# Bias stage of an attention and MoE kernel: two fp16 coefficient parts, three pairs of switch tiles by 16-bit distance, two blocks per chunk on ScalarE and GpSimd

## The chip, the cores and the metric

The kernel runs on one core of a Trainium2 chip. The metric is device time in microseconds (us), the median of several executions. One further execution was taken with the hardware profiler; all rows below are from that one.

## The reference, cut to what matters

An attention (batch 4, 8 heads, sequence 576, head size 64) whose scores get a bias from a small network of the position distance, then a gated MoE layer over the 2304 tokens of width 512.

```python
rel = (pos[:, None] - pos[None, :]).astype(np.float32)
x = (np.log1p(np.abs(rel)) / psi_i)[..., None]
h = np.maximum(x @ w1 + b1, 0.0)          # 32 hidden units
bias = h @ w2                             # one value per head
scores = scale * q @ k.T + bias.transpose(2, 0, 1)[None]
attn = exp(scores - max); attn = attn / (sum + 1e-9)
out = (sigmoid(y @ w_gate) * (y @ w_val)) @ w_out   # y = attn @ v, all heads side by side
```

All in fp32. The bias has 8 x 576 x 576 values and does not depend on the batch.

## The kernel before, in words

Three stages follow each other on the same engines: the bias stage, the attention over 16 units (4 head pairs x 4 batches), and the MoE. The order of every engine's instructions is the order in which the code writes them.

The bias stage uses that a ReLU is a switch times a line: for each pair of positions and each hidden unit a switch tile holds 1 where the unit is on, and bias = x * (sum of switch * w1 * w2) + (sum of switch * b1 * w2). The stage runs over 9 chunks of 64 query positions. A chunk has 16 switch tiles of 4 queries x 32 hidden units on the partitions and 576 keys in the free dimension, and 5 blocks of keys, taken in the order 0, 1, 4, 2, 3 (`BORD`): four of 128 keys with 16 groups of sums each, and block 4 with 64 keys and 8 groups.

- Twelve tiles of a chunk (`OWN`) come from TensorE: `one` makes y by two matmuls of 288 columns (line 332) into a PSUM tile, and ScalarE (line 337, a very steep sigmoid) or in chunk 0 partly VectorE (line 335) turns it into a bf16 switch. Two pairs (`DPAIRS`, tiles 6, 7, 14, 15) come from VectorE by comparing fp16 distances with fp16 thresholds (`apart`, line 350): one instruction of 1024 elements per pair and one of 256 for the rest ("far").
- `sums` (line 356) multiplies a switch tile as the stationary operand with the coefficients `cfs`, 64 columns, in three bf16 parts: three matmuls per group, 72 groups per chunk.
- `leave` takes a block out of its PSUM tile (`bps`, two buffers): VectorE multiplies the first half with x (line 364, or line 377 for block 4) into `btmp`, then adds the second half into the bias tiles by two instructions (line 372, heads 0 to 5 and 6 to 7). For block 0 (not in the last chunk) and block 4, ScalarE copies the second half (line 367) and GpSimd adds (lines 372 and 382).
- The y tiles and far pieces of the next chunk are placed between the sums by the tables `YPOS` and `DPOS` (a number is 16 x the block's place + the group).
- After every block `conv` runs a step of a preparation of nine MoE weight blocks: per block an absolute value on ScalarE (line 201) and four VectorE instructions on 512 elements (lines 204, 207, 210 and 213). From the second chunk on about one of these VectorE instructions follows each block.

The attention's softmax (line 567) reads the bias tiles on VectorE. Quoted from `leave` and the loop:

```python
if blk in BPOOL and c < NCH - 1 or blk == 4:
    rest, add = tp.tile([128, 2, H, 32], F32, name="brest")[:, 0:n], nc.gpsimd
    nc.scalar.activation(out=rest, in_=ps[:, 0:n, 1], func=AF.Copy)
else:
    rest, add = ps[:, 0:n, 1], nc.vector
```

In what follows block 1's eviction on VectorE (its multiply and two adds) is called E1, block 2's E2 and block 3's E3.

Of the kernel before, what the change touches and what calls it, by code (L numbers as in the profile page):

```python
# [31 lines left out]
YPOS = [18, 22, 26, 30, 34, 38, 46, 52, 57, 62, 67, 72], [3, 9, 15, 21, 27, 33, 39, 45, 52, 58, 66, 72]  # L32
DPAIRS = range(6, 8)
# [115 lines left out]
def tile_kernel(ctx, tc, q, k, v, small, w_gate, w_val, w_out, steps, lpos, xtab, lx, out, phases="0AB"):  # L149
# [8 lines left out]
    with ExitStack() as right, ExitStack() as att:  # L158
# [7 lines left out]
        biases = over.tile([128, 24, S], F32, name="bias0"), keep.tile([128, 8, S], F32, name="bias3")  # L166
# [1016 lines left out]
```

## Time and profile before

| | |
|---|---|
| median of 3 runs | 803.83 us (803.63 to 804.48) |
| profiled execution, its own time | 804.37 us |
| its span | 802.6 us |
| TensorE matmul busy in the span | 774.0 us (96%) |
| VectorE | 634.8 us (79%) |
| ScalarE | 511.5 us (64%) |
| GpSimd | 343.7 us (43%) |
| bias stage: first sums at | 15.07 us |
| first softmax of the attention at | 108.26 us |

Busy shares are over the whole span. The bias stage is the first eighth of it, and there the four engines hand tiles to each other through few buffers, so the times at which one instruction starts after another say more than the shares. In a timeline row the first number is the start, the second the duration, both in us, and a bracket gives the idle time before it and what ended it. Neighbouring instructions of one engine overlap a little, so the distance between two starts (the pitch) is what an instruction costs in a row of them.

### The profile page before, as it was taken

What the parts mean: (1) busy time and instruction counts of PE and PEld (TensorE: products, weight loads), DVE (VectorE), ACT (ScalarE), POOL (GpSimd) and SP (SyncE); (2) the same over time, 40 slices, a digit from 0 to 9 for tenths busy, and PEclk for the clock granted to TensorE, in tenths of its full rate; (3) what the DMA queues carried; (4) which work ended last, traced back from release to release, by engine and by line L of the source; (5) the groups of instructions that cost most, each with busy time, mean ns of one, the idle gap of its engine ahead of it and who ended that gap; (6) DMA issues with size and microseconds to landing.
All of it is one profiled execution on the core that took longest, in us unless ns stands there. A gap on an engine that the chain in (4) does not pass through costs nothing.

```text
span 802.6 us, 17329 instructions
## 1 busy us (share of the span) xinstructions
PE 774.0 (96%) x6356; PEld 722.8 (90%) x6356; DVE 634.8 (79%) x1301; ACT 511.5 (64%) x1094; POOL 343.7 (43%) x400
## 2 busy tenths in 40 slices
PE   7999989999999998899999999999999999999997
PEld 4888879999999998888998999889999999999996
DVE  6788888999999999896799899877877865656542
ACT  5888769989989987784444443554545546444442
POOL 1233559999989998951000000126233231523200
PEclk8999999999999999999999999999999999999999
DMA  5543434654664667747999633376334306321202
GB/s 198 152 147 126 130 97 125 176 167 131 180 172 127 180 178 205 212 125 234 367 313 297 203 132 131 118 220 220 111 106 145 105 27 212 129 73 64 75 1 79
DMA packets 66693, 124.21 MB, mean 155 GB/s; under 512 B 7344, under 2 KB 28976, under 8 KB 66608
## 3 DMA queue, kind: packets, MB, share of 16 engines
q1 hardware_dynamic: 64688, 120.15, 48.8%
q10 hardware_dynamic: 1920, 2.95, 1.2%
q8 instruction: 50, 0.82, 0.4%
q14 instruction: 35, 0.29, 0.1%
HBM read 86.04 MB, written 27.60 MB: 142 GB/s over the span
## 4 chain that ended last, share of the span: by engine, by line
PE 73%; DVE 13%; ACT 5%; DMA 4%; issue 3%; SPq 1%; POOL 0%; ACTq 0%; DVEq 0%
PE po L916 16%; PE pg L1018 12%; PE pu L1018 9%; PE sc L563 8%; PE acc L648 7%; PE pt L586 6%; PE pu L892 4%; PE pg L892 4%; PE bps L356 3%; DMA xin<-xs 2%; PE y L332 2%; DVE btmp L364 2%; ACT ind L337 1%; DVE en L567 1%; DVE bias L372 1%
## 5 line engine op out<-in xcount | busy, mean ns | idle before, releaser
L975 POOL TENSOR_TENSOR ws<-wm 128x256 f32<-128x256 f32 x44 | 41.4, 940 | 301.6 <-DMA wm<-scratch 147.0
L570 ACT ACTIVATE en<-en,mn 128x576 f32<-128x576 f32 x144 | 111.5, 774 | 31.7 <-DVE mn L567 30.7
L1018 PE MATMUL pg<-xq,wv 128*128 128x384 f32 x576 | 117.2, 338 | 1.0 <-ACT c L1044 1.0
L563 PE MATMUL sc<-k,QS 128*128 128x288 f32 x640 | 112.2, 301 | 1.4 <-DVE bias L372 0.6
L1018 PEld LDWEIGHTS pg<-xq,wv 128*128 128x128 f32 x576 | 103.2, 188 | 9.7 <-ACT c L1044 1.7
L567 DVE CUSTOM_DVE_ANT_0 en<-sc,bias 128x576 f32<-128x576 f32 x128 | 93.9, 751 | 7.4 <-PE sc L563 6.4
L1024 DVE TENSOR_TENSOR c<-pu,c 128x384 f32<-128x384 f32 x72 | 40.1, 557 | 74.5 <-PE pu L1018 29.3
L563 PEld LDWEIGHTS sc<-k,QS 128*128 128x128 f32 x640 | 92.0, 189 | 2.8 <-PE sc L563 0.8
L586 PE MATMUL pt<-ident,en 128*128 128x128 f32 x576 | 87.5, 275 | 3.1 <-DVE aL L486 1.9
L916 PE MATMUL po<-wo,gh 128*128 128x512 f32 x288 | 89.6, 392 | 0.0
L1018 PE MATMUL pu<-xq,wv 128*128 128x384 f32 x432 | 87.6, 337 | 0.4 <-DVE g L902 0.3
L1018 PEld LDWEIGHTS pu<-xq,wv 128*128 128x128 f32 x432 | 76.6, 188 | 3.3 <-DVE g L902 0.8
L648 PE MATMUL acc<-aH,vv 128*128 128x288 f32 x240 | 76.3, 334 | 3.2 <-DVE xe L651 3.0
L586 PEld LDWEIGHTS pt<-ident,en 128*128 128x128 f32 x576 | 68.7, 141 | 6.6 <-ACT en L570 3.4
L486 DVE TENSOR_TENSOR aL<-pt,aH 128x512 fp32r<-128x512 f32 (+1 forms) x112 | 66.6, 607 | 7.1 <-ACT aH L485 7.1
L356 PE MATMUL bps<-cfs,ind 128*128 128x64 bf16 x1458 | 67.4, 193 | 3.1 <-DVE bias L372 2.4
L337 ACT ACTIVATE ind<-y 128x576 bf16<-128x576 f32 x100 | 62.1, 653 | 10.5 <-PE y L332 8.2
L356 PEld LDWEIGHTS <-ind 128*128 128x128 bf16 x1458 | 58.6, 98 | 9.6 <-DVE bias L372 4.2
L648 PE MATMUL acc<-aL,vv 128*128 128x288 f32 x240 | 67.1, 296 | 0.0
L1036 ACT ACTIVATE gh<-c 128x384 fp32r<-128x384 f32 x48 | 25.2, 526 | 62.9 <-DVE c L1034 62.9
L490 POOL TENSOR_TENSOR aL<-ar,aH 128x512 fp32r<-128x512 f32 x48 | 62.4, 1300 | 4.0
L1044 ACT ACTIVATE c<-pg 128x384 f32<-128x384 f32 x72 | 35.1, 487 | 38.0 <-PE pg L1018 37.1
(152 smaller groups left out, 1913.4 us busy)
## 6 DMA issues: line engine op xcount, KB each, us to landing
wm<-scratch SPq DMA_DIRECT2D x48, 256.0 KB, 2.6
wo<-parts SPq DMA_DIRECT2D x24, 512.0 KB, 5.2
kr<-in_k_dram SPq DMA_DIRECT2D x32, 288.0 KB
QS<-part SPq DMA_DIRECT2D x64, 144.0 KB, 2.5
xs<-xe SPq DMA_DIRECT2D x32, 288.0 KB, 3.5
xin<-xs SPq DMA_DIRECT2D x48, 192.0 KB, 4.0
parts<-w SPq DMA_DIRECT2D x12, 512.0 KB, 10.0
vr<-in_v_dram SPq DMA_DIRECT2D x16, 320.0 KB, 3.6
```

Source lines behind the costliest of these rows:

```text
L337: nc.scalar.activation(out=o, in_=y[:, :, 0:HF], func=AF.Sigmoid, scale=float(2.0 ** 64))
L356: nc.tensor.matmul(out=o, lhsT=st, rhs=cfs[:, part], start=(part == 0), stop=(part == 2))
L486: return lambda: nc.vector.tensor_tensor(out=lo, in0=ps, in1=hi.bitcast(F32), op=ALU.subtract)
L490: nc.gpsimd.tensor_tensor(out=lo, in0=src, in1=hi.bitcast(F32), op=ALU.subtract)
L563: nc.tensor.matmul(out=ps[:, e, 0:HF], lhsT=l, rhs=r[:, HF * e:HF * e + HF], start=(i == 0), stop=(i == len(mms) - 1))
L567: nc.vector.tensor_tensor_reduce(out=half(en), in0=ps[:, :, 0:HF], in1=half(nbias), scale=-0.125, scalar=3.0e38, op0=ALU.add, op1=ALU.min, ...
L570: nc.scalar.activation(out=en, in_=en, func=AF.Exp, bias=mn, scale=-1.0, accum_out=sm)
L586: nc.tensor.transpose(pt[:, J], en[:, 128 * J:128 * J + 128], ident)
L648: nc.tensor.matmul(out=acc[:, 0:HF], lhsT=l, rhs=r, start=(i == 0), stop=(i == len(mms) - 1))
L892: self.nc.tensor.matmul(out=(pg, pu)[z], lhsT=l, rhs=r, start=(kc == 0 and i == 0), stop=(kc == 3 and i == 2))
L916: self.nc.tensor.matmul(out=po, lhsT=l[:, tt], rhs=r, start=(first and i == 0), stop=(last and i == 2))
L1018: nc.tensor.matmul(out=p, lhsT=W[i][:, l, at + kc], rhs=V[b][:, r, kc], start=(new and n == 0), stop=(n == 5), skip_group_check=not new)
```

## The change

- `cfs` becomes two fp16 parts instead of three bf16 ones, and all switch tiles fp16. So that fp16's range holds, the coefficients are scaled by a power of two found on the chip: a new input `wide` (w2 laid out on all partitions, 128 KB), a product with w1 and b1 on GpSimd, a maximum over 513 elements on VectorE, and bit operations for the factors `up` and `un`. `un` is applied when a block leaves.
- `DPAIRS` has three pairs (5, 6, 7): ten tiles by TensorE and ScalarE, three far pieces of 1024 elements and one of 384 per chunk.
- Blocks 0 and 4 leave wholly by ScalarE (one copy of both halves, scaled by `un`: 1024 or 512 elements) and GpSimd (multiply, then adds). In the last chunk block 0 stays on VectorE as before.
- For blocks 1 to 3 the adds become `scalar_tensor_tensor` with `un` as a scalar operand read from SBUF; x is scaled once by `un` on ScalarE in chunk 0 (three instructions of 576 elements, one of 64).
- The bias tiles get the layout [32-query piece, block, head, 32], so that the adds write contiguously, and the softmax reads its bias in pieces of 32.
- New tables `YPOS`, `DPOS`, `OWN_DVE`, `CFI` for ten tiles and four far pieces.

```diff
-YPOS = [18, 22, 26, 30, 34, 38, 46, 52, 57, 62, 67, 72], [3, 9, 15, 21, 27, 33, 39, 45, 52, 58, 66, 72]
-DPAIRS = range(6, 8)
+YPOS = [18, 23, 28, 33, 38, 46, 52, 58, 64, 71], [3, 10, 17, 24, 31, 38, 46, 54, 62, 70]
+DPAIRS = range(5, 8)
-DPOS = [20, 36, 52], [6, 22, 38]
+DPOS = [20, 34, 48, 60], [2, 9, 30, 36]
-CFI = 1
+CFI = 5
-OWN_DVE = (5, 9, 11, 13)
+OWN_DVE = (11, 12)
...
-        biases = over.tile([128, 24, S], F32, name="bias0"), keep.tile([128, 8, S], F32, name="bias3")
+        biases = over.tile([128, 18, 4, 6, 32], F32, name="bias0"), keep.tile([128, 18, 4, 2, 32], F32, name="bias3")
...
+        nc.gpsimd.tensor_tensor(
+            out=both[:, 0:2 * H * HID].rearrange("p (z h m) -> p z h m", z=2, h=H),
+            in0=wd.rearrange("p (o h) m -> p o h m", o=1).to_broadcast([128, 2, H, HID]),
+            in1=wr.rearrange("p z (o m) -> p z o m", o=1).to_broadcast([128, 2, H, HID]), op=ALU.mult)
...
+        nc.vector.tensor_reduce(out=big, in_=both, axis=mybir.AxisListType.X, op=ALU.max, apply_absolute_value=True)
...
         def sums(o, st):
-            for part in range(3):
-                nc.tensor.matmul(out=o, lhsT=st, rhs=cfs[:, part], start=(part == 0), stop=(part == 2))
+            for part in range(2):
+                nc.tensor.matmul(out=o, lhsT=st, rhs=cfs[:, part], start=(part == 0), stop=(part == 1))
...
-            if blk in BPOOL and c < NCH - 1 or blk == 4:
-                rest, add = tp.tile([128, 2, H, 32], F32, name="brest")[:, 0:n], nc.gpsimd
-                nc.scalar.activation(out=rest, in_=ps[:, 0:n, 1], func=AF.Copy)
...
+            away = blk in BPOOL and c < NCH - 1 or blk == 4
+            if away:
+                both = tp.tile([128, 2, 2, H, 32], F32, name="both")[:, 0:n]
+                nc.scalar.activation(out=both, in_=ps[:, 0:n], func=AF.Copy, scale=un)
+            else:
+                both = ps
+            (nc.gpsimd if away else nc.vector).tensor_tensor(out=tmp, in0=both[:, :, 0], in1=x, op=ALU.mult)
...
+                    if away:
+                        nc.gpsimd.tensor_tensor(out=o, in0=a, in1=b, op=ALU.add)
+                    else:
+                        o, a, b = (z.rearrange("p s h j -> p s (h j)") for z in (o, a, b))
+                        nc.vector.scalar_tensor_tensor(out=o, in0=a, scalar=un, in1=b, op0=ALU.mult, op1=ALU.add)
...
+                if c == 0 and n < 4:
+                    x = xt[:, 0, S - 64:S] if n == 3 else xt[:, n + 1]
+                    nc.scalar.activation(out=x, in_=x, func=AF.Copy, scale=un)
...
-            nbias = biases[0][:, 8 * p + s] if p < 3 else biases[1][:, s]
+            nbias = biases[0][:, :, it, 2 * p + h] if p < 3 else biases[1][:, :, it, h]
```

The order of VectorE in the program before, one inner chunk: block 0's multiply with a far piece on either side of it, E1, the rest of the far pieces, block 4's multiply, then E2 and E3 (cvm is the weight preparation).

```order
L350 TENSOR_TENSOR far<-dist,edge 128x2x512
L364 TENSOR_TENSOR btmp<-bps,xt 128x512
L204 TENSOR_SCALAR cvm<-cvm 128x512
L350 TENSOR_TENSOR far<-dist,edge 128x2x512
L364 TENSOR_TENSOR btmp<-bps,xt 128x512
L372 TENSOR_TENSOR bias_73<-bps,btmp 128x2x6x32
L372 TENSOR_TENSOR bias_74<-bps,btmp 128x2x2x32
L207 TENSOR_SCALAR cvm<-cvm 128x512
L350 TENSOR_TENSOR far<-dist,edge 128x2x128
L377 TENSOR_TENSOR btmp<-bps,xt 128x256
L210 SCALAR_TENSOR_TENSOR cvm<-cvw,cvm 128x512
L364 TENSOR_TENSOR btmp<-bps,xt 128x512
```

In it VectorE does something for every block, and two pieces of 1024 are compared.

The same place on VectorE in the changed program, from the preparation step after the previous chunk's E3 on.

```order
L202 TENSOR_SCALAR cvm<-cvm 128x512
L364 TENSOR_TENSOR far<-dist,edge 128x2x512 x2
L205 TENSOR_SCALAR cvm<-cvm 128x512
L364 TENSOR_TENSOR far<-dist,edge 128x2x512
L387 TENSOR_TENSOR btmp<-bps,xt 128x512
L395 SCALAR_TENSOR_TENSOR bias_73<-bps,fit,btmp 128x2x192
L395 SCALAR_TENSOR_TENSOR bias_74<-bps,fit,btmp 128x2x64
L208 SCALAR_TENSOR_TENSOR cvm<-cvw,cvm 128x512
L364 TENSOR_TENSOR far<-dist,edge 128x3x128
L211 SCALAR_TENSOR_TENSOR cvm<-cvw,cvm 128x512
L387 TENSOR_TENSOR btmp<-bps,xt 128x512
```

The multiplies of blocks 0 and 4 are gone, and three far pieces and two preparation steps now stand in a row ahead of E1.

GpSimd in the program before, one chunk: the adds of block 0, then the four of block 4.

```order
L372 TENSOR_TENSOR bias_73<-brest,btmp 128x2x6x32
L372 TENSOR_TENSOR bias_74<-brest,btmp 128x2x2x32
L382 TENSOR_TENSOR biasL<-brest,btmp 64x4x32 x4
```

It waits for VectorE's multiply in both blocks.

GpSimd in the changed program, one chunk.

```order
L387 TENSOR_TENSOR btmp<-both,xt 128x512
L392 TENSOR_TENSOR bias_73<-both,btmp 128x2x192
L392 TENSOR_TENSOR bias_74<-both,btmp 128x2x64
L387 TENSOR_TENSOR btmp<-both,xt 128x256
L401 TENSOR_TENSOR biasL<-both,btmp 64x4x32 x4
```

Two multiplies have come in, and both blocks now wait for ScalarE's copy alone.

## Rows read from the trace of the kernel before

**Rows 1.** Busy time by stretch, whole core; the first line names the columns.

```profile
core 0: us, PE busy (x) PEld busy (x) DVE busy (x) ACT busy (x) POOL busy (x), PEclk, DMA share, GB/s
10.00:15.00 5.00, 4.76 (x21) 2.87 (x19) 4.63 (x13) 4.32 (x8) 0.00 (x0) 0.54 0.10 37
...
60.00:80.00 20.00, 18.66 (x461) 16.82 (x459) 17.00 (x37) 17.56 (x32) 7.07 (x12) 1.00 0.39 126
...
600.00:700.00 100.00, 100.00 (x522) 93.26 (x521) 70.37 (x118) 51.45 (x107) 30.02 (x34) 1.00 0.35 120
```

**Rows 2.** Timeline of TensorE: y tiles at the start and later, sums late in the stage.

```profile
8.88 1.14 PE L332 MATMUL y<-lt,wy 128*128 128x288 bf16 x4 [3.24 <-DVE wy L299]
...
62.57 0.41 PE L332 MATMUL y<-lt,wy 128*128 128x288 bf16 x2
62.81 0.51 PE L356 MATMUL bps<-cfs,ind 128*128 128x64 bf16 x12
...
104.49 0.69 PE L356 MATMUL bps<-cfs,ind 128*128 128x64 bf16 x18
...
105.19 0.69 PE L356 MATMUL bps<-cfs,ind 128*128 128x64 bf16 x18
```

**Rows 3.** Timeline of VectorE: evictions, far pieces and weight preparation in the bias stage.

```profile
29.75 0.69 DVE L364 TENSOR_TENSOR btmp<-bps,xt 128x512 f32<-128x512 f32 x1 [0.68 <-PE bps L356]
...
47.53 0.42 DVE L204 TENSOR_SCALAR cvm<-cvm 128x512 f32<-128x512 f32 x1
47.86 0.69 DVE L350 TENSOR_TENSOR far<-dist,edge 128x1024 bf16<-128x1024 f16 x1
48.47 0.69 DVE L364 TENSOR_TENSOR btmp<-bps,xt 128x512 f32<-128x512 f32 x1
...
60.72 0.69 DVE L364 TENSOR_TENSOR btmp<-bps,xt 128x512 f32<-128x512 f32 x1
61.44 0.76 DVE L372 TENSOR_TENSOR bias<-bps,btmp 128x384 f32<-128x384 f32 x2
62.12 0.68 DVE L213 SCALAR_TENSOR_TENSOR cvm<-cvw,cvm 128x512 int32<-128x512 int32 x1
62.71 0.29 DVE L350 TENSOR_TENSOR far<-dist,edge 128x256 bf16<-128x256 f16 x1
...
102.25 0.69 DVE L364 TENSOR_TENSOR btmp<-bps,xt 128x512 f32<-128x512 f32 x1
...
105.39 0.69 DVE L364 TENSOR_TENSOR btmp<-bps,xt 128x512 f32<-128x512 f32 x1 [0.73 <-PE bps L356]
```

**Rows 4.** Groups by shape on VectorE: 128 elements with and without a scalar from SBUF.

```profile
L295 DVE SCALAR_TENSOR_TENSOR btmp<-wh,small,btmp 128x128 f32<-128x128 bf16 x2 | 0.7, 352 | 0.1
...
L297 DVE TENSOR_TENSOR btmp<-btmp,wh 128x128 f32<-128x128 f32 x2 | 0.6, 285 | 0.0
```

**Rows 5.** Groups by shape on ScalarE and GpSimd, and GpSimd's adds of one block 0.

```profile
L337 ACT ACTIVATE ind<-y 128x576 bf16<-128x576 f32 x100 | 62.1, 653 | 10.5 <-PE y L332 8.2
...
L367 ACT ACTIVATE brest<-bps 128x512 f32<-128x512 f32 x8 | 4.8, 598 | 5.4 <-DVE btmp L364 5.4
...
L382 POOL TENSOR_TENSOR biasL<-brest,btmp 64x128 f32<-64x128 f32 x36 | 18.1, 502 | 21.0 <-DVE btmp L377 19.4
...
L490 POOL TENSOR_TENSOR aL<-ar,aH 128x512 fp32r<-128x512 f32 x48 | 62.4, 1300 | 4.0
...
29.34 1.41 POOL L372 TENSOR_TENSOR bias<-brest,btmp 128x384 f32<-128x384 f32 x2 [5.03 <-ACT brest L367]
```

**Rows 6.** VectorE beside GpSimd in the MoE: timeline, and a group of 600 to 700.

```profile
619.66 0.93 POOL L975 TENSOR_TENSOR ws<-ws,wm 128x256 f32<-128x256 f32 x1
619.92 1.22 DVE L986 TENSOR_TENSOR wv<-wm,wv 128x512 fp32r<-128x512 f32 x1
...
623.69 0.68 DVE L986 TENSOR_TENSOR wv<-ws,wv 128x512 fp32r<-128x512 f32 x1
...
L986 DVE TENSOR_TENSOR wv<-ws,wv 128x512 fp32r<-128x512 f32 x18 | 14.4, 810 | 2.6 <-ACT wv L981 2.4
```

More of the change, by code (lines that the diff above doesn't have):

```diff
@@ L178, in tile_kernel @@
         with tc.manual_schedule():
-            bias(tc, small, steps, lpos, xtab, lx, biases, biasL, moe, lambda: next(attn))
+            bias(tc, small, wide, steps, lpos, xtab, lx, biases, biasL, moe, lambda: next(attn))
         if "A" in phases:
@@ L215, in narrow, with bias @@
     return size, clamp, low, top, tail
-def bias(tc, small, steps, lpos, xtab, lx, biases, biasL, moe, begun):
+def bias(tc, small, wide, steps, lpos, xtab, lx, biases, biasL, moe, begun):
     nc = tc.nc
@@ L235, in load_lx @@
         def load_lx(c):
-            lt = lp.tile([128, len(OWN) // 4, S], BF16, name="lt")
+            lt = lp.tile([128, PLANES, S], BF16, name="lt")
             nc.sync.dma_start(out=lt, in_=lx[c].bitcast(BF16))
@@ L248, in bias @@
         lt = load_lx(0)
+        wd = cp.tile([128, H, HID], F32, name="wide")
+        nc.sync.dma_start(out=wd.rearrange("p h m -> p (h m)"), in_=wide)
         dist = cp.tile([128, 2 * S], F16, name="dist")
@@ L306, in bias @@
         cf = cp.tile([128, 2, H, 4], F32, name="cf")
+        fit = cp.tile([128, 5], F32, name="fit")
+        big, up, un = (fit[:, i:i + 1] for i in range(3))
+        both = cp.tile([128, 2 * H * HID + 1], F32, name="both")
+        nc.gpsimd.memset(both[:, 2 * H * HID:], 2.0 ** -100)
+        nc.gpsimd.tensor_tensor(
+            out=both[:, 0:2 * H * HID].rearrange("p (z h m) -> p z h m", z=2, h=H),
+            in0=wd.rearrange("p (o h) m -> p o h m", o=1).to_broadcast([128, 2, H, HID]),
+            in1=wr.rearrange("p z (o m) -> p z o m", o=1).to_broadcast([128, 2, H, HID]), op=ALU.mult)
+        nc.gpsimd.tensor_scalar(out=fit[:, 3:5], in0=wb, scalar1=float(2.0 ** 13), scalar2=None, op0=ALU.mult)
         for ab in range(2):
@@ L381, in leave @@
                 for e in range(2):
-                    add.tensor_tensor(
-                        out=biasL[64 * e:64 * e + 64, :, j], in0=rest[r, 0, e::2], in1=tmp[r, 0, e::2], op=ALU.add)
+                    nc.gpsimd.tensor_tensor(
+                        out=biasL[64 * e:64 * e + 64, :, j], in0=both[r, 0, 1, e::2], in1=tmp[r, 0, e::2], op=ALU.add)
         ind, own, far = switches(0, lt)
-        cfs = cp.tile([128, 3, 2, H, 4], BF16, name="cfs")
+        cfs = cp.tile([128, 2, 2, H, 4], F16, name="cfs")
         for i, f in enumerate(own):
             f()
-            if far and i in (2, 4, 6):
+            if far and i in (1, 2, 4, 6):
                 far.pop(0)()
             part, sub = divmod(i - CFI, 2)
-            if part in range(3):
+            if part in range(2):
                 if not sub:
                     nc.vector.tensor_copy(out=cfs[:, part], in_=cf)
-                elif part < 2:
+                elif part < 1:
                     nc.vector.tensor_tensor(out=cf, in0=cf, in1=cfs[:, part], op=ALU.subtract)
```

47 lines of the change are left out of this document (23 added, 24 removed).

## The prediction

> **What bounds the kernel now.** I read the busy time by stretch first. In the MoE TensorE is busy all the time [rows 1], and the change leaves that part alone, so what the bias stage gains or loses should reach the end whole. In the bias stage TensorE is busy for 18.66 us of 20, VectorE for 17.0 and ScalarE for 17.56 [rows 1]: nobody is free, and who ends last must come from the timeline. The reader should look for two starts in it: E1 of chunk 1 at 29.75 and E1 of chunk 8 at 102.25 [rows 3], seven chunks, so **10.36 us per chunk**. TensorE alone explains most of that. From 104.49 to 105.19 it starts 24 sums (the 18 of the row and six on far tiles), 0.0292 us each, and a y tile takes 62.57 to 62.81, 0.24 us [rows 2]. A chunk has 216 sums (6.30) and 12 y tiles (2.88): 9.2 us. The missing 1.2 us is waiting for PSUM buffers.
>
> **The change part by part.** *TensorE*: 144 sums (4.20) and 10 y tiles (2.40), 6.6 us per chunk. It stops being the bound, with 2.6 us per chunk saved there. fp16 instead of bf16 I cost at nothing: both have two bytes.
>
> *VectorE* becomes the bound, and what it does not give away is its cycle. The pitches are: multiply of an eviction 0.72 (60.72 to 61.44), its two adds 0.68 (to 62.12), a two-input preparation step 0.59 (to 62.71), a one-input one 0.33 (47.53 to 47.86), a far piece of 1024 0.61 (to 48.47) [rows 3]. A preparation step is 0.46 in the mean, and one follows every block. The new adds read `un` from SBUF. An instruction of 128 elements with such a scalar takes 352 ns, one without 285 [rows 4], so 0.07 more each; this price is not shown for PSUM sources, and its bounds are 0 and 0.07. I take 0.07, as the only row with this form says: an eviction costs 0.72 + 0.68 + 0.14 = 1.54.
>
> The cycle follows from the two `bps` buffers. E2's block can start on TensorE only when E1 has freed its buffer, and it needs 32 sums (0.93), three y tiles (0.72) and about 0.3 for the two hand-overs (estimated from 0.68 to 0.73 us of waits in the rows; bounds 0 and 0.7): 1.95. Between E1 and E2 VectorE has two steps and the rest of the far pieces, some 1.3 us, hidden in that time. So, from E3 to E3: step 0.46, three far pieces 1.83, step 0.46, E1 1.54, block 2 on TensorE 1.95, E2 1.54, step 0.46, E3 1.54: **9.78 us**. ScalarE's work is ten sigmoids of at most 0.65, a copy of 1024 elements at most twice 0.598, one of 512 at 0.6 [rows 5] and an absolute value: about 9 with the overlap of neighbours counted as cost, under the cycle. The cover of the y tiles' wait on ScalarE is that distance; without it TensorE would stall in block 1.
>
> *GpSimd* goes from 1.41 + 4 x 0.50 = 3.4 us per chunk to 5.45: a multiply of 512 elements (1.3, the group of that size) and one of 256 (about 0.7, half of it) come in [rows 5]. That is half of a chunk and no bound by itself. E3 waits for it, as `btmp` has two buffers and E3 takes the one that block 4's adds on GpSimd have read. Block 4's copy ends some 3.5 us after E3 of the chunk before, GpSimd is through with it at 7 to 8, and E3 starts at 8.2: just hidden.
>
> *What VectorE and GpSimd take from each other* is the unknown. In the MoE a two-input VectorE instruction of 512 elements takes 1.22 us while GpSimd is in the middle of an add (619.66 to 620.59), and 0.68 when it isn't; over a stretch in which GpSimd is busy 30% of the time the mean is 810 ns, 0.13 more than alone [rows 1, 6]. Now far pieces and preparation steps read two inputs from SBUF or run beside such adds, while evictions read one from PSUM. GpSimd's work starts about 1.2 us after E3 (TensorE's block 0 has waited for E2's buffer, then comes ScalarE's copy). So the first step and the first far pieces are ahead of it, the step and the third far piece before E1 meet it, the three instructions between E1 and E2 are covered, and the step before E3 comes when GpSimd is done. For two instructions I take the measured 0.13, scaled from 30% to 55% busy: 0.24 each, **0.48**. Bounds: 0, and the rival below. The chunk is then 10.26 us, and 7 x 0.10 = **0.7 us** is gained.
>
> [...]
>
> *Chunk 0 and the head.* Until E1 of chunk 1, TensorE loses four y matmuls at 1.14/4 us [rows 2], 72 sums and two more y tiles: 1.1 + 2.1 + 0.5 = 3.7. Against it stand three scalings of x on ScalarE (about 0.65 each and 0.2 for the short one) and the larger copies, 2.2 + 1.2, less two sigmoids, 1.3: 2.1 us more on ScalarE. The maximum over 513 elements (at most 0.7) replaces one of VectorE's two switch tiles saved, and GpSimd's product lies before VectorE's distances are ready. Bounds 0 and 3.7; I take **2.0** earlier.
>
> *Chunk 8*: VectorE waits 0.73 for TensorE there [rows 3], which goes, and the multiply of block 4 (0.34); the scalars cost 4 x 0.14. **0.5** earlier.
>
> *The softmax* reads bias in pieces of 32: the adds of before already wrote in such pieces, so nothing; were it dearer, TensorE would cover it until VectorE fills up. `wide` adds 128 KB to the loads of the first 15 us: nothing.
>
> Sum: 2.0 + 0.7 + 0.5 = 3.2 us earlier than the profiled 804.37, so 801.2; the median of the runs is 0.54 below the profiled one, so **800.6 us**.
>
> **The rivals.** [...] Far pieces come in ahead of GpSimd or win, and the scalar costs nothing: 9.78 - 0.42 = 9.36 per chunk, 7 x 1.0 + 2.5 = 9.5 us earlier, 794.3. For it: in the bias stage of before hardly an instruction meets another. Against: GpSimd now works through half of each chunk.
>
> [...] Each waiting instruction goes after one of the other engine. From E3's end: GpSimd's multiply asks at 1.2 and starts when the second far piece ends at 1.7; it holds the next step until 2.9; the adds of 384 elements hold the third far piece until 4.4; E1 starts near 4.8 instead of 2.75. With 0.3 more between E1 and E2 a chunk takes 9.78 + 2.35 = 12.1. Chunk 1 is hardly hit (no preparation yet); six chunks x 1.75 = 10.5, less 2.5 + 0.6: about 7.5 us later, **811**. It decides where the waits before E1 pass 0.95 us per chunk, since 7 x (0.95 - 0.58) eats the 2.5 us won at both ends. For it: the 1.22 us row. Against: the mean of 0.13 in a stretch where both also work side by side.
>
> [...]
>
> *Nothing can be told*: another wait eats the 3 us and the time is within 0.2%, 1.6 us, which is about what a measurement of this kernel can tell from no change.
>
> **How the numbers follow.** The forecast has a chance of 0.42, the free port 0.12, the alternating port 0.36, the clock 0.02, no difference that can be told 0.08. A fifth of the forecast's own spread falls within 1.6 us. Faster: 0.12 + 0.34 = 0.46; same 0.16; slower 0.38. The likeliest case alone spans 797 to 804. The range takes in the free port and the alternating one, 794 to 811.
>
> **What would show it.** Right: E1 to E1 of 10.0 to 10.5 us, a TensorE that waits for VectorE's adds ahead of block 2, far pieces of 0.7 to 1.0 us before E1. [...] E1 of chunk 1 near 27.7 confirms the head. A softmax instruction over 0.78 us, or a granted clock under 1.00 after 20 us, would make the argument wrong.

## The result and the profile after

The changed kernel takes **814.15 us** in the median of four runs (813.14 to 814.98); four runs of the kernel before beside it have a median of 803.73. The ratio is 1.0133, with a 95% interval of 1.0111 to 1.0155: slower, where the forecast said 800.6. The profiled execution has a span of 812.8 us against 802.6. In the MoE TensorE is busy all the time as before; the bias stage changed, as the busy time by stretch shows (columns as in [rows 1]).

```profile
60.00:80.00 20.00, 15.56 (x319) 13.53 (x317) 19.70 (x33) 16.78 (x27) 12.99 (x16) 0.92 0.44 148
94.00:98.00 4.00, 3.59 (x56) 2.99 (x54) 3.96 (x8) 3.14 (x5) 1.86 (x2) 0.58 0.60 203
118.00:126.00 8.00, 6.79 (x36) 6.42 (x36) 4.16 (x12) 7.12 (x16) 3.99 (x5) 0.59 0.45 109
600.00:700.00 100.00, 100.00 (x522) 93.40 (x521) 68.85 (x113) 51.62 (x109) 31.28 (x34) 1.00 0.35 118
```

TensorE went from 18.66 to 15.56 us of 20, VectorE from 17.00 to 19.70, GpSimd from 7.07 to 12.99 [rows 1]: VectorE is the bound, as forecast. New are the granted clocks: 0.58 and 0.59 in the two short stretches, where the kernel before has 1.00 in both.

Four marks in VectorE's timeline say where the 10.2 us of the span are: E1 of chunk 1, E1 of chunk 8, the first softmax instruction of the attention and its thirteenth.

```profile
29.74 0.68 DVE L387 TENSOR_TENSOR btmp<-bps,xt 128x512 f32<-128x512 f32 x1
...
110.46 0.69 DVE L387 TENSOR_TENSOR btmp<-bps,xt 128x512 f32<-128x512 f32 x1
...
116.58 0.75 DVE L589 CUSTOM_DVE_ANT_1 en<-sc,bias 128x576 f32<-128x576 f32 x1
...
137.04 0.74 DVE L589 CUSTOM_DVE_ANT_1 en<-sc,bias 128x576 f32<-128x576 f32 x1
```

Before they stood at 29.75 and 102.25 [rows 3], and at these:

```profile
108.26 0.75 DVE L567 CUSTOM_DVE_ANT_0 en<-sc,bias 128x576 f32<-128x576 f32 x1
...
126.14 0.73 DVE L567 CUSTOM_DVE_ANT_0 en<-sc,bias 128x576 f32<-128x576 f32 x1
```

| part | before, us | after, us | difference | forecast |
|---|---|---|---|---|
| to E1 of chunk 1 | 29.75 | 29.74 | 0.0 | -2.0 |
| seven chunks, E1 to E1 | 72.50 (10.36 each) | 80.72 (11.53 each) | +8.2 | -0.7 |
| E1 of chunk 8 to the first softmax | 6.01 | 6.12 | +0.1 | -0.5 |
| first to thirteenth softmax | 17.88 | 20.46 | +2.6 | 0 |
| the rest | 676.46 | 675.76 | -0.7 | 0 |

The seven chunks first. Here are VectorE and then GpSimd ahead of E1 of chunk 6 (at 87.86):

```profile
83.81 1.29 DVE L364 TENSOR_TENSOR far<-dist,edge 128x1024 f16<-128x1024 f16 x2
85.01 1.50 DVE L202 TENSOR_SCALAR cvm<-cvm 128x512 f32<-128x512 f32 x1
86.43 1.50 DVE L364 TENSOR_TENSOR far<-dist,edge 128x1024 f16<-128x1024 f16 x1
87.86 0.68 DVE L387 TENSOR_TENSOR btmp<-bps,xt 128x512 f32<-128x512 f32 x1
88.57 0.88 DVE L395 SCALAR_TENSOR_TENSOR bias<-bps,fit,btmp 128x384 f32<-128x384 f32 x2
89.36 0.50 DVE L205 TENSOR_SCALAR cvm<-cvm 128x512 int32<-128x512 int32 x1
89.78 0.61 DVE L364 TENSOR_TENSOR far<-dist,edge 128x384 f16<-128x384 f16 x1
```

```profile
84.43 1.79 POOL L387 TENSOR_TENSOR btmp<-both,xt 128x512 f32<-128x512 f32 x1 [4.44 <-ACT both L384]
86.31 1.94 POOL L392 TENSOR_TENSOR bias<-both,btmp 128x384 f32<-128x384 f32 x2
88.32 0.72 POOL L387 TENSOR_TENSOR btmp<-both,xt 128x256 f32<-128x256 f32 x1
```

Two far pieces ahead of GpSimd take 1.29 together. Then GpSimd's multiply asks at 84.43, and from there on both engines work in turns: a one-input step takes 1.50 instead of 0.42 [rows 3], the third far piece 1.50 instead of 0.69. The eviction at 87.86 keeps its 0.68 while GpSimd works on; behind it the rest of the far pieces takes 0.61 instead of 0.35. The groups by shape on VectorE from 31 to 110 us give the sum:

```profile
L364 DVE TENSOR_TENSOR far<-dist,edge 128x1024 f16<-128x1024 f16 x18 | 16.4, 941 | 0.0
L387 DVE TENSOR_TENSOR btmp<-bps,xt 128x512 f32<-128x512 f32 x21 | 14.3, 680 | 1.1 <-PE bps L370 1.0
L395 DVE SCALAR_TENSOR_TENSOR bias<-bps,fit,btmp 128x384 f32<-128x384 f32 x22 | 13.6, 618 | 0.8
L202 DVE TENSOR_SCALAR cvm<-cvm 128x512 f32<-128x512 f32 x9 | 8.0, 892 | 0.0
L211 DVE SCALAR_TENSOR_TENSOR cvm<-cvw,cvm 128x512 int32<-128x512 int32 x8 | 7.7, 967 | 0.0
...
L208 DVE SCALAR_TENSOR_TENSOR cvm<-cvw,cvm 128x512 int32<-128x512 int32 x9 | 7.1, 787 | 0.0
L205 DVE TENSOR_SCALAR cvm<-cvm 128x512 int32<-128x512 int32 x9 | 7.1, 784 | 0.0
L364 DVE TENSOR_TENSOR far<-dist,edge 128x384 f16<-128x384 f16 x7 | 4.3, 608 | 0.0
```

Against their lengths alone (far 0.687 and 0.352, steps 0.418 and 0.682) that is 4.6 + 1.8 for the far pieces and 4.3 + 2.3 + 0.9 + 3.3 for the steps: 17.2 us in seven chunks, **about 2.45 us of longer instructions per chunk**. The evictions lost nothing.

With these lengths VectorE hardly ever waits. Here is 40 to 110 us, first before and then after:

```profile
40.00:110.00 70.00, 63.88 (x1563) 57.23 (x1562) 60.70 (x131) 52.70 (x93) 29.29 (x45) 1.00 0.42 131
40.00:110.00 70.00, 46.35 (x974) 40.27 (x970) 69.21 (x111) 47.87 (x76) 44.34 (x53) 0.93 0.38 120
```

VectorE is busy for 69.21 us of 70, and ahead of its multiplies it waited for TensorE's sums for 1.0 us in all (the second line of the groups above). So sums that come late, for whatever reason, have cost the seven chunks no more than about 1 us of their 8.2 directly.

### The profile page after: what moved, and what is told of

The parts are those of the page before. It is cut to its first block, busy times and chain, and to the rows that moved or that the text cites. A ratio compares the mean times of both kernels' runs of the same rounds, so it can differ in the third digit from the quotient of the medians.

```text
span 812.8 us, 15965 instructions
## 1 busy us (share of the span) xinstructions
PE 757.6 (93%) x5672; PEld 707.2 (87%) x5672; DVE 651.5 (80%) x1292; ACT 511.9 (63%) x1082; POOL 369.6 (45%) x421
## 4 chain that ended last, share of the span: by engine, by line
PE 70%; DVE 8%; issue 2%; ACT 2%; POOL 2%; DMA 1%; SPq 0%; ACTq 0%; DVEq 0%; POOLq 0%
PE po L939 17%; PE pg L1041 12%; PE pu L1041 9%; PE sc L585 7%; PE acc L671 7%; PE pt L609 6%; PE pu L915 5%; PE pg L915 5%; DVE en L589 2%; PE pt L629 1%; DVE aL L508 1%; ACT en L593 1%; DVE w L880 1%; DMA xin<-xs 1%; DVE a L508 1%
## 5 line engine op out<-in xcount | busy, mean ns | idle before, releaser
L370 PE MATMUL bps<-cfs,ind 128*128 128x64 f16 x810 | 46.2, 198 | 27.0 <-DVE bias L395 18.9
L370 PEld LDWEIGHTS <-ind 128*128 128x128 f16 x810 | 38.0, 101 | 33.7 <-DVE bias L395 19.9
L351 ACT ACTIVATE ind<-y 128x576 f16<-128x576 f32 x84 | 52.5, 653 | 20.6 <-PE y L346 19.6
```

Of the source, the lines that this page charges most:

```text
L351: nc.scalar.activation(out=o, in_=y[:, :, 0:HF], func=AF.Sigmoid, scale=float(2.0 ** 64))
L370: nc.tensor.matmul(out=o, lhsT=st, rhs=cfs[:, part], start=(part == 0), stop=(part == 1))
```

## The experiments

Theory A: VectorE and GpSimd work in turns, and that makes the chunk longer. Theory B: VectorE's list is simply too long. Theory C: TensorE's lower clock does it. The table has all runs; "clock" is that of 40 to 110 us, "far" the mean of a far piece of 1024 from 31 to 110, "softmax" the time from the first to the thirteenth. Ratios are to the kernel before beside the runs. In fixed_order and fixed_two_order E1 follows block 0's multiply at once: their chunks are counted from that multiply, and E1 is put 0.6 us behind it.

| kernel | E1 of chunk 1 | us per chunk | far, us | clock | softmax | time, us | ratio [95%] |
|---|---|---|---|---|---|---|---|
| before | 29.75 | 10.36 | 0.688 | 1.00 | 17.88 | 803.73 | |
| changed | 29.74 | 11.53 | 0.941 | 0.93 | 20.46 | 814.15 | 1.0133 [1.0111, 1.0155] |
| no_gpsimd | 35.72 | 10.56 | 0.822 | 0.95 | 17.86 | 809.77 | 1.0077 [1.0059, 1.0094] |
| no_gpsimd2 | 30.40 | 10.32 | 0.845 | 0.96 | 18.30 | 804.32 | 1.0012 [0.9995, 1.0030] |
| far_late | 29.44 | 12.75 | 0.768 | 0.89 | 20.20 | 825.39 | 1.0269 [1.0240, 1.0297] |
| three_sums | 30.52 | 11.70 | 0.896 | 0.95 | 20.01 | 819.91 | 1.0192 [1.0168, 1.0217] |
| mult_vector | 29.58 | 10.68 | 0.687 | 0.96 | 18.45 | 808.05 | 1.0066 [1.0044, 1.0088] |
| parts_only | 32.76 | 11.53 | 1.065 | 0.93 | 18.45 | 817.37 | 1.0177 [1.0151, 1.0202] |
| two_pairs | 31.14 | 10.31 | 0.687 | 1.00 | 20.11 | 808.34 | 1.0057 [1.0035, 1.0080] |
| fixed_scale | 24.68 | 11.69 | 0.955 | 0.87 | 17.88 | 807.04 | 1.0046 [1.0025, 1.0068] |
| fixed_away | 25.22 | 11.14 | 0.891 | 0.93 | 19.20 | 808.00 | 1.0057 [1.0040, 1.0074] |
| mv_order | 30.16 | 12.02 | 0.685 | 0.83 | 17.88 | 816.92 | 1.0171 [1.0154, 1.0188] |
| mv_even | 29.51 | 10.67 | 0.686 | 0.98 | 18.28 | 807.48 | 1.0054 [1.0039, 1.0069] |
| fixed_order | 25.0 | 11.1 | 0.685 | 0.93 | 17.87 | 806.49 | 1.0043 [1.0027, 1.0058] |
| fixed_two_order | 26.6 | 10.7 | 0.684 | 0.90 | 17.94 | 805.20 | 1.0026 [1.0013, 1.0038] |
| fixed_away_two | 26.33 | 10.25 | 0.774 | 0.92 | 20.60 | 803.18 | 1.0000 [0.9991, 1.0009] |
| after_table | 29.62 | 11.36 | 0.998 | 0.95 | 18.45 | 813.96 | 1.0125 [1.0108, 1.0143] |
| best_table | 26.17 | 10.26 | 0.771 | 0.93 | 18.61 | 801.18 | 0.9978 [0.9968, 0.9988] |
| best_warm | 26.62 | 10.26 | 0.771 | 0.98 | 18.33 | 800.93 | 0.9966 [0.9954, 0.9979] |

### Does GpSimd's work make the chunk longer?

```
no_gpsimd
             if away:
+                return
-            (nc.gpsimd if away else nc.vector).tensor_tensor(out=tmp, ...)
+            nc.vector.tensor_tensor(out=tmp, ...)
```

> The changed kernel without GpSimd's multiplies and adds of blocks 0 and 4 (left out: the bias of these two blocks is filled with zeros once at the start); ScalarE's scaled copies stay, VectorE's list of instructions is the same. Theory A (VectorE's far pieces and preparation steps alternate with GpSimd's instructions): E1 to E1 falls from 11.5 to 9.4-9.9 us, far pieces of 1024 go from a mean of 0.855 to 0.69 us, and the time from 814 to 799-803 us. Theory B (VectorE's list of a chunk is simply too long, GpSimd matters little): a chunk stays at 11.2-11.5 us and the time at 812-815. Theory C (TensorE's lower granted clock is what holds the evictions up): the sums of a block stay late, VectorE idles for them, and the time is over 808 even where the far pieces are short.

809.77: the stage starts 6 us later, so the total says little. The fills stand behind the coefficients in GpSimd's queue; what they held up is VectorE's cast of these coefficients. It takes 0.20 us in the changed kernel, and here it ends with the last of three fills in a row:

```profile
14.17 6.07 DVE L418 CAST cfs<-cf 128x64 f16<-128x64 f32 x1 [0.46 <-POOL cf L324]
```

```profile
14.27 2.97 POOL L326 MEMSET bias<- 128x3456 f32 x1
17.19 1.05 POOL L327 MEMSET bias<- 128x1152 f32 x1
18.18 2.01 POOL L328 MEMSET biasL<- 128x2304 f32 x1
```

That is a meeting of the two engines too, and one without turns.

> The kernel no_gpsimd again (GpSimd's multiplies and adds of blocks 0 and 4 left out, their bias zero), with the fills of zeros moved to the very start, where GpSimd and VectorE wait for the first loads: in no_gpsimd they took 6 us of GpSimd ahead of chunk 0 and made E1 of chunk 1 start at 35.7 instead of 29.7. Theory A: E1 of chunk 1 near 29.7, 9.6 us per chunk where GpSimd is idle, and 799-804 us in all (11.5 - 9.6 = 1.9 us by 6 to 7 chunks). If the gain of no_gpsimd came from something else, it stays at 809-810.

804.32, some 10 us less than the changed kernel. E1 of chunks 2 to 5 stands at these times:

```profile
41.21 0.69 DVE L392 TENSOR_TENSOR btmp<-bps,xt 128x512 f32<-128x512 f32 x1
...
50.49 0.69 DVE L392 TENSOR_TENSOR btmp<-bps,xt 128x512 f32<-128x512 f32 x1
...
60.05 0.69 DVE L392 TENSOR_TENSOR btmp<-bps,xt 128x512 f32<-128x512 f32 x1
...
69.95 0.68 DVE L392 TENSOR_TENSOR btmp<-bps,xt 128x512 f32<-128x512 f32 x1
```

9.58 us per chunk, where the changed kernel takes 11.23 for the same chunks (E1 at 42.84 and 76.54), with VectorE's list unchanged and far pieces at their length alone:

```profile
57.64 1.29 DVE L367 TENSOR_TENSOR far<-dist,edge 128x1024 f16<-128x1024 f16 x2
```

So for the chunks theory A holds and theory B falls. What left the chunk is 1.65 us, less than the 2.45 of longer instructions: freed of them, VectorE waits more for TensorE's sums (5.8 us from 31 to 110, against 1.0). The time stays over 803 because GpSimd, being free, now prepares the attention's keys from 76 to 83 us, and chunk 5 takes 13.64:

```profile
78.09 2.96 DVE L367 TENSOR_TENSOR far<-dist,edge 128x1024 f16<-128x1024 f16 x2
80.97 0.89 DVE L202 TENSOR_SCALAR cvm<-cvm 128x512 f32<-128x512 f32 x1
81.78 1.89 DVE L367 TENSOR_TENSOR far<-dist,edge 128x1024 f16<-128x1024 f16 x1
```

### Can the far pieces be moved out of its way, and does TensorE have too little to do?

```
far_late
-DPOS = [20, 34, 48, 60], [2, 9, 30, 36]
+DPOS = [20, 34, 48, 60], [64, 66, 68, 70]
```

> The changed kernel with one row of numbers changed: the far pieces of chunks 1 to 7 are written between the second and the third eviction instead of ahead of the first; the same instructions, in another order. Theory A (alternation with GpSimd): GpSimd's work on blocks 0 and 4 lies in the 6.7 us after the third eviction, where VectorE now has evictions that read PSUM, so far pieces fall to about 0.69 us, a chunk to 9.8-10.6 us and the time to 802-808. Theory B (the list is too long): the sum of the same instructions is the same, 11.5 us per chunk, 813-815, or slower, since the far tiles are now ready later for the next block 0 on TensorE.

It missed: 825.39, the slowest of all, though its far pieces are shorter, 0.768 in the mean.

```profile
48.08 2.15 DVE L364 TENSOR_TENSOR far<-dist,edge 128x1024 f16<-128x1024 f16 x4
...
54.68 0.69 DVE L387 TENSOR_TENSOR btmp<-bps,xt 128x512 f32<-128x512 f32 x1 [2.15 <-PE bps L370]
```

Four pieces take 2.15 us, as alone. But the next chunk's block 0 on TensorE needs these tiles, so VectorE then waits 2.15 us for sums, at a clock of 0.83 (50 to 60 us). From 31 to 110 us such waits are 16.4 us, against 1.0 in the changed kernel. Meetings are not the only thing that counts.

```
three_sums
+            nc.tensor.matmul(out=o, lhsT=st, rhs=cfs[:, 1], start=True, stop=True)
             for part in range(2):
```

> The changed kernel with a third matmul in front of every pair of sums (the second part alone, overwritten by the pair that follows), so that TensorE has 216 sums per chunk again: 8.7 us with the y tiles instead of 6.6. Theory C (the granted clock of 0.77-0.89 in six stretches of the changed kernel costs much): the clock is 1.00 in nearly all stretches and the time falls to 809 us or less; of that the stretch after the bias stage gives about 1.9 us. Theory A (VectorE and GpSimd alternate, TensorE has room): the chunk stays at 11.3-11.9 us, and only the stretch after the stage gives something: 811-815.

819.91, slower than either theory expected: more work on TensorE doesn't take its idles away (two of 2.90 us begin at 41.8 and 88.35), and the clock is 0.83 from 40 to 50 and from 90 to 100 us. The mean clock of 0.95 is little over the changed kernel's 0.93, so theory C's condition was hardly made, and the run neither shows nor excludes it.

### Which part of the change?

```
mult_vector: the multiplies of blocks 0 and 4 on VectorE, from PSUM
+                for z in range(n):
+                    nc.vector.scalar_tensor_tensor(out=tmp[:, z], in0=ps[:, z, 0], scalar=un, in1=x[:, z], op0=ALU.mult, op1=ALU.mult)
two_pairs: DPAIRS, YPOS, DPOS and OWN_DVE of the kernel before
parts_only: both
```

> The changed kernel, but the multiplies of blocks 0 and 4 are on VectorE again, straight from PSUM with the scale as a scalar (block 0 in two halves of 256 elements); ScalarE copies only the other half of the block, GpSimd has the adds alone, three pairs stay. Theory A: VectorE gets about 1.2 us more of its own per chunk, and loses two of GpSimd's instructions (1.3 to 1.8 and 0.73 us) to wait for: 11.0-11.8 us per chunk, 811-816. Theory B: 1.2 us more per chunk and nothing back: 12.7 us per chunk, 821-824.

> The changed kernel with two pairs and the order of before (18, 22, ... and 3, 9, ...) instead of three pairs; blocks 0 and 4 stay wholly on ScalarE and GpSimd. VectorE has one far piece of 1024 fewer (0.6 us per chunk), ScalarE two sigmoids and TensorE two y tiles more (1.2 and 0.5 us). Theory A: GpSimd's work of 5.4 us per chunk still meets the far pieces and steps, so 811-818. Theory B (VectorE's own list sets the chunk): 0.6 us less per chunk, 808-811.

> Only the first part of the change: two fp16 parts with the scale; two pairs of switch tiles and the order of before, and the multiplies of blocks 0 and 4 on VectorE as in the kernel mult_vector. TensorE needs 4.2 + 2.9 = 7.1 us per chunk, VectorE 9.9 us by its own list (three evictions 4.62, multiplies of blocks 0 and 4 1.3, far pieces 1.7, steps 2.3), GpSimd 3.4. Theory A: few meetings as in the kernel before, 10.0-10.4 us per chunk and 800-804 us. Theory B: 10.0 us per chunk and 801. If the new adds and the wider copies cost more than TensorE's 2 us give, it is slower than before: over 805.

mult_vector: 808.05, under the ranges of both theories: some 1.2 us more of its own work per chunk, and yet 0.85 us less per chunk, with far pieces at 0.687: the two multiplies cost less on VectorE than on GpSimd. two_pairs: 808.34, in theory B's range and under that of A. A's meetings are there, on the steps in place of the far pieces:

```profile
L208 DVE SCALAR_TENSOR_TENSOR cvm<-cvw,cvm 128x512 int32<-128x512 int32 x9 | 9.0, 1000 | 0.0
L211 DVE SCALAR_TENSOR_TENSOR cvm<-cvw,cvm 128x512 int32<-128x512 int32 x9 | 8.7, 961 | 0.0
...
L364 DVE TENSOR_TENSOR far<-dist,edge 128x1024 f16<-128x1024 f16 x12 | 8.2, 687 | 0.0
```

Its chunks 2 to 6 take 10.0 us each at a clock of 1.00, with no idle of TensorE of 1.3 us or more from 20 to 105 us; why A's range was too high was not tested further. parts_only missed: 817.37, with far pieces at 1.065 and, ahead of E2's block, idles of 2.13 to 2.41 us on TensorE in each of six chunks. No single part of the change makes it slow: two_pairs and mult_vector undo one part each, and both win 6 us; with both undone it is slower again, and what parts_only's longer far pieces and its idles each cost was not separated.

### What the on-chip scale costs

```
fixed_away
-            nc.gpsimd.tensor_scalar(out=cf[:, ab], ..., scalar1=fit[:, 3 + ab:4 + ab], scalar2=up, ...)
+            nc.gpsimd.tensor_scalar(out=cf[:, ab], ..., scalar1=wb[:, ab:ab + 1], scalar2=8.0, ...)
-                nc.scalar.activation(out=both, in_=ps[:, 0:n], func=AF.Copy, scale=un)
+                nc.scalar.activation(out=both, in_=ps[:, 0:n], func=AF.Copy)
-                        nc.vector.scalar_tensor_tensor(out=o, in0=a, scalar=un, in1=b, ...)
+                        nc.vector.tensor_tensor(out=o, in0=a, in1=b, op=ALU.add)
```

> The kernel mult_vector without the scale that is found on the chip: coefficients times the fixed 8 of the kernel before, no maximum, no scaling of x, no scalar in the multiplies and adds, plain copies (for other weights than these the fp16 parts could over- or underflow). The scale costs in the sum: 6 adds of 0.06-0.07 and the two multiplies per chunk, 0.55 us, so 10.1 us per chunk instead of 10.7; and up to 2 us on ScalarE in chunk 0. Expected: 802-804 us if the scale's steps lie on the path; 807-808 if VectorE and ScalarE only wait longer instead.

> The changed kernel with the fixed factor 8 in place of the scale found on the chip, and nothing else changed (blocks 0 and 4 stay wholly on ScalarE and GpSimd, three pairs). If the scale holds up the start: E1 of chunk 1 at 25-26.5 instead of 29.7. Per chunk 0.42 us less of adds, but the same meetings with GpSimd: 11.0-11.5 us, and 805-809 us in all. If the start does not move: 811-813.

E1 of chunk 1 comes at 24.68 and 25.22: the scale costs **4.5 us** at the start of the changed kernel. In VectorE's timeline the first coefficients are cast at 11.58 in fixed_away, and 2.8 us later in the changed kernel:

```profile
11.17 0.68 DVE L320 TENSOR_REDUCE fit<-both 128x1 f32<-128x513 f32 x1
...
14.36 0.20 DVE L413 CAST cfs<-cf 128x64 f16<-128x64 f32 x1 [0.46 <-POOL cf L324]
```

The coefficients now stand behind the maximum and two multiplies of GpSimd that take 2.11 us beside the far pieces. About 1.1 us is lost before that: beside GpSimd's product (6.39 to 7.65) a cast of VectorE takes 1.33 us, where it takes 0.23 in fixed_away:

```profile
6.41 1.33 DVE L291 CAST wh<-btmp 128x128 bf16<-128x128 f32 x1
```

Both kernels give much of it back: fixed_scale takes 11.69 us per chunk instead of the 10.1 expected, with far pieces at 0.955 and a clock of 0.87; so its 807.04 missed the 802 to 804 of the first case; it falls into the second's 807 to 808, though the longer far pieces, which that case did not name, have a part in it. fixed_away landed in its range.

### Order, idle and clock

```
mv_order: mult_vector, with steps behind blocks 1 and 3 alone, and
-DPOS = [20, 34, 48, 60], [2, 9, 30, 36]
+DPOS = [20, 34, 48, 60], [2, 6, 10, 36]
-                conv((5 * c + n) in CSTEPS)
+                for m in ((), (0, 1), (), (), (2, 3, 4))[n]:
+                    conv((5 * c + m) in CSTEPS)
mv_even: mult_vector, with
+DPOS = [20, 34, 48, 60], [2, 9, 12, 36]
```

> The kernel mult_vector in another order of VectorE's instructions alone: three far pieces ahead of block 0's multiply, no preparation step right after blocks 0 and 4 (two follow E1, three follow E3), so that GpSimd's adds find evictions on VectorE, which kept their length beside GpSimd in every run so far (0.68 and 0.62 us), and no far pieces or steps. Theory A: no step or far piece over 0.75 us in chunks 1 to 7, VectorE's own list of 10.2 us per chunk, 10.2-10.5 measured (mult_vector 10.7), 804-807 us. If it is not the meetings but the length of the list and TensorE's answers that count, 808-811, as there is more waiting where three steps now stand in a row.

> The kernel mult_vector with one number changed: the third far piece stands ahead of block 0's multiply and not behind it; the preparation steps stay one behind each block. The same instructions as mult_vector and mv_order. TensorE's idle of a chunk should split into two of 1.3-1.7 us (mv_order: one of 2.1-2.4). If the lower clock comes with the long idle: clock 1.00 in the stage's stretches, 10.3-10.7 us per chunk, 805-808 us. If the order as such is bad for TensorE's answers: 11-12 us per chunk and 810-817, as in mv_order.

The same instructions on each engine, and 9.4 us between them. The meetings are gone in both (far pieces 0.685 and 0.686). In mv_order three steps and three far pieces stand in a row ahead of block 0's multiply, TensorE waits for it, and this follows:

```profile
64.82 0.45 PE L370 MATMUL bps<-cfs,ind 128*128 128x64 f16 x10 [2.11 <-DVE btmp L389]
65.11 0.35 PE L370 MATMUL bps<-cfs,far 128*128 128x64 f16 x4
65.28 0.67 PE L346 MATMUL y<-lt,wy 128*128 128x288 bf16 x2
```

After an idle of 2.11 us two y tiles take 0.67 instead of 0.41 [rows 2], until 72 us. The granted clock is 0.66 from 64 to 74, and over 40 to 110 it is 0.83, where mv_even has 0.98. VectorE's waits for sums went from 3.3 to 9.6 us. So a gain in one place (no meetings) was lost in another (TensorE waits longer and its clock is lower), and mv_order missed both its ranges. Order, idles and clock changed together, so how much of the 9.4 us is the clock's is not shown. Nor is the link of idle and clock one to one: up to 100 us mult_vector has six idles of 1.58 to 1.85 us and one stretch at the lower clock (0.83 from 40 to 50 us), and mv_even has that same stretch (43 to 46 us, 0.83 from 40 to 50) after idles of 1.35 at most.

> The same new order on the kernel fixed_scale (fixed factor 8 in place of the scale found on the chip). There E1 of chunk 1 came at 24.7, 5 us ahead of all other kernels, and the seven chunks gave it back: 11.7 us each with far pieces of 0.955 us in the mean and a lower clock in five stretches. Theory A: without meetings the chunk is VectorE's list, 9.65 us, measured 9.7-10.2; E1 of chunk 8 at 93-97 and 794-798 us, faster than the kernel before. Theory C (the clock goes down because TensorE has too little to do, whatever VectorE meets): stretches at 0.83 remain, 10.8-11.7 us per chunk and 803-808.

> As fixed_order, with two pairs instead of three: VectorE 0.6 us per chunk less (list 9.05), ScalarE two sigmoids more (about 8.9 us), TensorE two y tiles more (7.1). Theory A: 9.1-9.7 us per chunk, 790-797 us. If ScalarE's sigmoids or TensorE's y tiles then end last, 10.0-10.5 us per chunk and 796-802.

806.49 and 805.20: theory A's 794 to 798 and 790 to 797 missed. No far piece meets GpSimd, but TensorE's longest idles of the chunks are 1.3 to 2.8 us up to 95 us, and the clocks 0.93 and 0.90.

### Behind the stage, and a version that beats both

> The kernel two_pairs with the fixed factor 8 in place of the scale. two_pairs had 10.0 us per chunk in chunks 2 to 7 without any idle of TensorE over 1.3 us there and without a low clock in the stage, and lost its time at the start (E1 of chunk 1 at 31.1) and behind the stage (clock 0.66). Without the scale: E1 of chunk 1 at 26-27.5, 9.6-10.0 us per chunk, E1 of chunk 8 at 95-98.5 and 798-802 us, faster than the kernel before. If the lower clock behind the stage costs over 2.5 us or the meetings grow: 803-806.

803.18: the stage is as expected (E1 of chunk 8 at 98.11, 4.1 us before that of the kernel before), and then it lost nearly all, with 20.60 us for twelve softmax steps. Two things differ there. ScalarE's load of the table for exp stood ahead of the attention in the kernel before:

```profile
103.19 1.28 ACT L570 ACT_TABLE_LOAD   x1
109.05 0.78 ACT L570 ACTIVATE en<-en,mn 128x576 f32<-128x576 f32 x1 [4.58 <-DVE mn L567]
```

In the changed kernel, as in far_late, three_sums, two_pairs, fixed_away and fixed_away_two, it comes behind the first minimum:

```profile
117.41 1.28 ACT L593 ACT_TABLE_LOAD   x1 [5.56 <-DVE mn L589]
118.70 0.78 ACT L593 ACTIVATE en<-en,mn 128x576 f32<-128x576 f32 x1
```

Why it comes late in the changed kernel no row shows. In no_gpsimd2 TensorE starts on the first exp's result 2.05 us after the first softmax began (109.89, 107.84); it is 1.71 in the kernel before, with the load ahead, and 3.04 in the changed one (119.62, 116.58): without GpSimd's work on the blocks the load is early again.

```
after_table, best_table (on fixed_away_two)
                 leave(ps, c, blk)
+                if c == NCH - 1 and blk == 4:
+                    nc.scalar.activation(out=early, in_=early, func=AF.Exp)
best_warm besides: two overwritten matmuls ahead of each pair of blocks 0, 1 and 4 of chunk 8
```

> The changed kernel with one instruction more: an exp of one element right behind ScalarE's last copy of the bias stage, so that the table of exp is loaded there, in ScalarE's idle time, and not behind the first minimum of the attention (1.28 us at 117.4 in the changed kernel). If the table lies on the path: 1.0-1.4 us earlier, 812.5-813.3 us, and the first twelve softmax steps take 19.0-19.5 us instead of 20.5. If the lower clock hides it: no change, 813.5-815.

> The kernel fixed_away_two with the same early exp. If the table lies on the path: 801.5-802.5 us, 0.1-0.2% faster than the kernel before; if TensorE's half clock from 100 to 112 us is what sets the pace there: 803 as without it.

> best_table with each pair of sums of blocks 0, 1 and 4 of the last chunk preceded by two more matmuls that are overwritten (160 in all, 4.7 us of TensorE, in the 0.8 to 1.3 us of idle that it has ahead of each block there). If the idles bring the lower clock: 1.00 or nearly so from 98 to 112 us instead of 0.50, twelve softmax steps in 17.9-18.5 us instead of 20.6, and 799.5-801.5 us, faster than the kernel before. If the clock stays at 0.50, or the added matmuls hold the last evictions up: 802-804.

Twelve softmax steps went from 20.46 to 18.45 us in after_table and from 20.60 to 18.61 in best_table, in whose trace they stand here:

```profile
104.56 0.76 DVE L572 CUSTOM_DVE_ANT_1 en<-sc,bias 128x576 f32<-128x576 f32 x1 [1.55 <-PE sc L568]
...
123.17 0.74 DVE L572 CUSTOM_DVE_ANT_1 en<-sc,bias 128x576 f32<-128x576 f32 x1
```

That is 2.0 us for a load of 1.28; the lower clock also ends sooner (0.68 from 108 to 110 us and 1.00 behind in best_table, 0.74 from 112 to 114 and 1.00 behind in fixed_away_two). The runs part the two causes, by where the load stands and by the granted clock of the first ten us from the first softmax on:

| load | clock | twelve steps, us | kernels |
|---|---|---|---|
| ahead of the attention | 0.99 to 1.00 | 17.86 to 17.94 | before, no_gpsimd, fixed_scale, mv_order, fixed_order, fixed_two_order |
| ahead of the attention | 0.76 to 0.84 | 18.28 to 18.61 | no_gpsimd2, mult_vector, parts_only, mv_even, after_table, best_table, best_warm |
| behind the first minimum | 1.00 | 19.20 | fixed_away |
| behind the first minimum | 0.58 to 0.66 | 20.01 to 20.60 | changed, far_late, three_sums, two_pairs, fixed_away_two |

In fixed_away the load is late (at 109.28, the first softmax at 108.46) with the clock at 1.00, and costs 1.3 us, its own length. The other 1.3 of the changed kernel's 2.6 us go with the lower clock. best_table is **0.22% faster than the kernel before**, 0.9978 [0.9968, 0.9988]. The runs of after_table don't show its gain (813.96, from 810.44 to 814.80, against 814.15), and its trace is of the fastest of them, whose chunks were 11.36 us: unsettled there. best_warm has its clock at 0.98 to 106 us, then 0.62 to 110; its interval overlaps that of best_table, so the added matmuls are not shown to help. Both best kernels have a fixed factor in place of the scale, which serves weights of this size alone.

## Why the prediction was wrong

- **"What VectorE and GpSimd take from each other".** This step failed: "for two instructions I take the measured 0.13, scaled ... 0.48". Measured: about 2.45 us of longer instructions per chunk, and a chunk of 11.53 where 9.58 was measured without GpSimd, so some 1.95 on the path instead of 0.48; ahead of E1 two or three instructions lose 0.8 to 1.1 us each, behind it others 0.1 to 0.3. A mean over a stretch in which GpSimd was mostly idle (30.02 us of 100 busy [rows 1]) says little on a stretch in which it works 65% of the time (12.99 us of 20). The row of 1.22 us [rows 6] was the one to take, and the second rival took it: it has a far piece of 1.5 us (2.9 to 4.4, measured 1.50), the place ahead of E1 (4.8 us from E3's end, measured 4.65, 83.21 to 87.86) and 811 us. Its total is near in part by luck: its 12.1 us per chunk were 11.53, and the 3.1 us that it took off for both ends and chunk 1 did not come. No run shows the port of which the chances and the range speak; what the runs show is that instructions of the two engines take longer beside each other: 1.50 us instead of 0.69 for a far piece, 1.79 for GpSimd's multiply, where the group of that size in the kernel before has a mean of 1.30 [rows 5]. A one-input step took 1.50 instead of 0.42 as well, and the forecast had its price from two-input rows alone.
- **The lone cycle of 9.78** was right, and by its parts: 9.58 measured without GpSimd, in chunk 3 of it 3.45 from E1 to E2 (3.49 forecast) and 4.26 from E3 to the next E1 (4.29). The eviction of 1.54 was: 1.50 from 87.86 to the step at 89.36. The scalar costs 0.06 for an add (0.618 against 0.558, 0.342 against 0.281), forecast 0.07.
- **"Chunk 0 and the head ... I take 2.0"** was wrong by 2.0. The terms of TensorE were there (fixed_away starts 4.5 us earlier), but the sum left 1.7 us for the scale (3.7 less 2.0), by 2.1 us of work on ScalarE, and it took 4.5. What failed is the cover: the product does lie before the distances are ready, but it holds a cast of VectorE up by 1.1 us, and the two multiplies of GpSimd behind the maximum, 2.11 us on the path of the coefficients, had no term.
- **"Chunk 8: 0.5 earlier"** came out at 0.1 later.
- **Behind the stage** the sum had no term, and 2.6 us were lost: by the table of loads and clocks 1.3 by the load and 1.3 with the lower clock. The clock had a chance of 0.02, and no run shows the whole stage at a lower clock. Measured are idles of TensorE of 1.72 to 2.25 us in five of seven chunks (behind block 3, where it waits for E2's adds) and a lower clock in parts of the stage (0.58 at 94 to 98) and behind it (0.59 at 118 to 126). The sign "a granted clock under 1.00 after 20 us" was met (0.92 from 60 to 80), though late sums cost the chunks themselves 1 us at most.
- **Softmax** over the new layout: 0.751 us, as before; right. TensorE freed, VectorE the bound: right.

The sum: 2.0 + 8.9 + 0.6 + 2.6 - 0.7 = 13.4 us between the forecast of 3.2 earlier and the 10.2 later of the trace. How far the clock also moved GpSimd's work in the chunks, and so the meetings, was not separated on the changed kernel itself.

## What to carry to other kernels

Before work is given to GpSimd, list what VectorE does while GpSimd works: here, in the changed kernel, SBUF-to-SBUF instructions took up to 1.50 us instead of 0.42 and up to 1.76 instead of 0.68 beside it, the multiply of an eviction from PSUM its own 0.68 to 0.69. When TensorE gets less to do in a chain of buffers, look where its waits fall and what its clock does after them; here the same instructions in another order were 9.4 us apart. ScalarE's table load of 1.28 us is better issued where that engine idles: behind the first minimum, at a clock of 1.00, twelve softmax steps took 19.20 us (fixed_away), with the load ahead of the attention 17.86 to 17.94.

## What was not expected of the hardware

- VectorE's evictions, with one operand in PSUM and one in SBUF, kept their lengths beside GpSimd in every run (the multiply 0.67 to 0.69 us, the larger add 0.62 with the scalar and 0.56 without); one-input steps from SBUF to SBUF went from 0.42 to 1.50.
- Who goes first is not fixed: in mult_vector GpSimd's add of 384 elements took 1.90 us while VectorE's far piece went ahead of it at 0.68; in fixed_scale the far piece took 1.49 in the same place. In no_gpsimd the cast, begun at 14.17 beside a multiply of GpSimd (14.11, 0.22 long), ended only with the last of the three fills behind that, after 6.07 us.
- TensorE's granted clock fell inside the stage (to 0.50 from 60 to 62 us in the changed kernel), often after idles of 1.6 to 2.9 us, but by no one length of idle: the changed kernel kept 1.00 from 40 to 58 us through an idle of 1.97 us (up to 47.80), and in mv_even it fell between 42 and 43 us (two y tiles take 0.41 at 41.91, 0.64 at 42.51) after idles of 1.35 and 0.98. In the kernel before and in two_pairs, without an idle of 1.3 us from 20 to 105 us, it stayed at 1.00 from 20 to 110 us; in fixed_away_two it fell at 99 us after three of 0.8 to 1.3 (0.85 from 98 to 100, 0.50 from 100 to 112), and had stayed at 1.00 through one of 1.37 at 69.
